# Attention probabilities turned by VectorE squares of 32 and DRAM transfers instead of by TensorE, from the fourth unit on

## The chip, the cores and the metric

One core of a Trainium2 chip runs the whole program. The metric is the device time of one execution in microseconds (us); lower is better. A time is the median of several runs; a profile is one execution recorded instruction by instruction.

## The reference

The program computes banded attention, and feeds its output to a gated feed-forward block with an RMS norm in front of it.

```python
# q, k, v: 8 batches x 8 heads x 576 rows x 64, float32
scores = (q @ k.T) / sqrt(64)
# heads 0-3: keep 0 <= rel < 32;  heads 4-7: keep 0 <= rel < 128 and rel % 4 == 0, with rel = row - key
attn = exp(scores - max);  attn = attn / (sum(attn) + 1e-9)
x = (attn @ v)                        # to 4608 tokens x 512
xn = x / sqrt(mean(x * x) + 1e-6) * rms_g
out = (silu(xn @ w_gate) * (xn @ w_val)) @ w_out      # 512 -> 1536 -> 512
```

## The kernel before, in words

**Units and bursts.** The 4608 tokens are cut into 16 units of 288 rows (half a sequence each, `U`). The attention of a unit is 14 bursts, `bursts(u)`: a burst is a pair of heads and a block of query rows. `geometry` gives its shape: pairs 0 and 1 (`c < 2`) have 3 blocks of 96 queries against 128 keys (96 keys for the first block of an even unit); pairs 2 and 3, the heads with dilation, have 4 blocks of 72 queries against 72 keys (even units) or 104 (odd units). From the fourth unit on (`u >= NEX`, 13 units, 182 bursts) the products of the attention are made in a high and a low part (float32r), so as to keep float32's accuracy.

**Steps.** The feed-forward block of a unit has 12 slices (`NJ`), and each slice three steps: `gate` (12 matmuls), `val` (12 matmuls) and `proj` of the slice before (12 matmuls). So a unit has 36 steps, and these matmuls fill TensorE. While unit u's feed-forward runs, the attention of unit u+1 is made in the gaps: `plan` writes down at which steps the parts of each burst go, and `attend` issues them behind the 12 matmuls of that step. From the fourth unit on the scores of burst k go at step -11 + 2k of the unit before, so one burst is started in every second step, 14 bursts in 28 of the 36 steps.

**What one burst does.** Let its scores be made at step s.

- s: `products` issues two score matmuls (L524) into the PSUM bank `s`.
- s+1: `scores_max` on VectorE: L381 adds the mask to the low part, L386 (twice) adds the rest and finds the maximum; the result is the tile `t`, 96 partitions x 2 heads x 128. The tag `t` has 3 buffers.
- s+2: `scores_exp` on ScalarE (L401), with the sums.
- s+4: `scores_norm`: two small operations on VectorE (L410, L411) and two multiplications on GpSimd (L417).
- s+6: two TensorE transposes (L497) into a free piece of a PSUM bank.
- s+7, s+8: `untranspose`: ScalarE copies the high part to the tile `pt` (L477), VectorE subtracts to get the low part (L479). The tag `pt` has 2 buffers.
- s+10: two output matmuls (L512) of `pt` with the parts of v into the bank `o`.
- s+11: `take` on VectorE (L439 and L441, twice each) adds the four pieces and moves them to `xraw`.

**What sets the order.** The schedule is manual: each engine runs its instructions in the order in which the program issues them. `later(dt, rank, fn)` puts a piece of work off by dt steps; `flush` at the start of a step issues what is due, sorted by rank; after it come the step's feed-forward matmuls and then `attend`. VectorE also carries two operations of each feed-forward slice (L724 behind `gate`, L737 behind `val`) in the same queue, and a `gate` two steps behind a `val` writes to that `val`'s PSUM bank, so it must wait for L737. All transfers are issued from one queue, SP's, in program order: `load` and `load_v` (L293, L301) for the next heads and value blocks, and the output (L777). A new tile in a slot waits until everything that used the tile before it in that slot is done, transfers included.

Of the kernel before, what the change touches and what calls it, by code (L numbers as in the profile page):

```python
# [20 lines left out]
P = 128  # L21
# [34 lines left out]
          2: (-3, -2, 0, 1, 3, 4, 6, 7, 9, 10, 12, 13, 15, 16)}  # L56

EARLY, LAST = -11, 15
BEHIND = 6, 10
DONE = 25  # L60


# [15 lines left out]
def attn_moe(ctx: ExitStack, tc: tile.TileContext, qk_in, v_in, w_gate, w_val, w_out, rms_g, outT):  # L78
# [6 lines left out]
    cst = ctx.enter_context(tc.tile_pool(name="cst", bufs=1))  # L85
    sb = ctx.enter_context(tc.tile_pool(name="sb", bufs=2))
    ps = ctx.enter_context(tc.tile_pool(name="ps", bufs=1, space=PSUM))


    ident = cst.tile([QB, QB], F32, name="ident")  # L90
# [29 lines left out]
    def later(dt, rank, fn):  # L120
        put_off.setdefault(now[0] + dt, []).append((rank, fn))
# [208 lines left out]
    def after(u, h, n):  # L330

        k = u * H + h + n
        return divmod(k, H) if k < NU * H else None
# [40 lines left out]
    def scores_max(u, c, i, s_ps):  # L374
        blocks, nq, _ = geometry(u, c)
        _, _, mc, n = blocks[i]
        sv = s_ps[:QB].rearrange("q (a t k) -> q a t k", a=2, t=2)
        other = u < NNAT and everything.index((u, c, i)) % 4 == 3
        t = sb.tile([QB, 2, P], F32, tag="qs" if other else "t", name=f"t_{u}_{c}_{i}", bufs=3)
        if u >= NEX:  # L380
            V.tensor_tensor(out=t[:nq, :, :n], in0=sv[:nq, :, 1, :n],  # L381
                            in1=mask[:nq, None, mc:mc + n].to_broadcast([nq, 2, n]), op=ALU.add)
        sm = sums[everything.index((u, c, i)) % len(sums)]
        for a in range(2):
            plus = t[:nq, a, :n] if u >= NEX else mask[:nq, mc:mc + n]
            V.tensor_tensor_reduce(out=t[:nq, a, :n], in0=sv[:nq, a, 0, :n], in1=plus,  # L386
                                   op0=ALU.add, op1=ALU.min,
                                   scale=-(0.5 if u == NNAT else 1.0) / math.sqrt(D),
                                   scalar=3e38, accum_out=sm[:nq, a, 0:1])
        st[u, c, i] = t, sm  # L390
# [77 lines left out]

    everything = [b for u in range(NU) for b in bursts(u)]

    def untranspose(b, t_ps, wait):
        blocks, nq, _ = geometry(*b[:2])
        n = blocks[b[2]][3]
        t_in = t_ps[:n].rearrange("k (a q) -> k a q", a=2)[:, :, :nq]
        exact = b[0] < NEX
        st[b] = pt = sb.tile([P, 2, 2, QB], F32 if exact else F32R, tag="pt", name=f"pt_{b[0]}_{b[1]}_{b[2]}", bufs=2)
        A.copy(out=pt[:n, 0, :, :nq], in_=t_in)  # L477
        def low_part():
            V.tensor_tensor(out=pt[:n, 1, :, :nq], in0=t_in, in1=pt[:n, 0, :, :nq], op=ALU.subtract)  # L479

        if not exact:
            later(1, 0.4 if wait > 1 else -1.5, low_part) if wait else low_part()

    def products(q, t, o, t_ps, s_tag="s", o_tag="o", wait=0):


        if q:
            s_ps = ps.tile([P, 512], F32, tag=s_tag, name=f"s_{q[0]}_{q[1]}_{q[2]}")
        if o:
            o_ps = ps.tile([P, 512], F32, tag=o_tag, name=f"o_{o[0]}_{o[1]}_{o[2]}")  # L490
            pt = st.pop(o)
        if t:
            p, _ = st.pop(t)
        def transposed(a):
            blocks, nq, _ = geometry(*t[:2])
            n = blocks[t[2]][3]
            PE.transpose(t_ps[:n, a * QB:a * QB + nq], p[:nq, a, :n], ident[:nq, :nq])  # L497

        def output(a):
            blocks, nq, _ = geometry(*o[:2])  # L500
            n = blocks[o[2]][3]
            if o[0] < NEX:
                if o[0] == 0:
                    PE.matmul(o_ps[a * D:(a + 1) * D, :nq], vs[o][:n, a], pt[:n, 0, a, :nq], start=True, stop=True)
                    return
                if a:
                    return
                out = o_ps[:, :2 * nq].rearrange("d (a q) -> d a q", a=2)
                PE.matmul(out, vs.pop(o)[:n].rearrange("k a d -> k (a d)"), pt[:n, 0, :, :nq], start=True, stop=True)  # L509
                return  # L510
            vp = vparts[everything.index(o) % 2]
            PE.matmul(o_ps[:, 2 * a * nq:2 * (a + 1) * nq].rearrange("d (t q) -> d t q", t=2),  # L512
                      vp[:n, a].rearrange("k t d -> k (t d)"), pt[:n, :, a, :nq], start=True, stop=True)

        def scored(a):
            blocks, nq, _ = geometry(*q[:2])
            qc, kc, _, n = blocks[q[2]]
            sv = s_ps[:QB].rearrange("q (a t k) -> q a t k", a=2, t=2)
            if q[0] < NEX:
                qk = heads[q[0], 2 * q[1] + a]  # L520
                PE.matmul(sv[:nq, a, 0, :n], qk[:, qc:qc + nq], qk[:, U + kc:U + kc + n], start=True, stop=True)  # L521
                return
            qs, ks = heads[q[0], 2 * q[1] + a]
            PE.matmul(sv[:nq, a, :, :n], qs[:, qc:qc + nq], ks[:, :, kc:kc + n], start=True, stop=True)  # L524

        order = ((t, transposed), (o, output), (q, scored))
        if t and t[0] >= NEX:
            order = ((o, output), (t, transposed), (q, scored))
        parts = [(b, fn, a) for b, fn in order for a in range(2)]
        for b, fn, a in parts:  # L530
            if b:
                fn(a)
        if t:
            later(1, 0.2, lambda: untranspose(t, t_ps, wait))
        if o:
            if o[0] < NEX or wait:
                later(1, 0.41 if o[0] < NEX else 0.55, lambda: take(*o, o_ps))
            else:
                for a in range(2):
                    later(1, (0.1, 0.3)[a], lambda a=a: take(*o, o_ps, (a,)))  # L540
            if o[0] < NEX:
                later(1, 9, lambda: load_v(further(o, 3)))
            far = further(o, 2)
            if far and far[0] >= NEX:
                split_v(far, 8 if o[0] < NEX else 1)
        if q:
            later(1, 0.7, lambda: scores_max(*q, s_ps))
            behind = q == (1, 0, 2)
            later(3 if behind else 2, 0.3 if behind else 0.42 if wait == 1 else 2, lambda: scores_exp(*q))
            later(3 if q[0] < NNAT else 4, 1 if behind else -1, lambda: scores_norm(*q))  # L550
            u, c, i = q
            nxt = after(u, 2 * c, 2)
            nb = len(geometry(u, c)[0])
            if u < NEX:
                if u == NNAT - 1 and c == NC - 1 and i == nb - 1:
                    for h in range(4):
                        later(1, 9, lambda h=h: load(NNAT, h))
                if u >= NNAT and i == nb - 1 and c < NC - 1:
                    for a in range(2):
                        later(1, 9, lambda a=a: load(*after(u, 2 * c + a, 4)))  # L560
                if u == NEX - 1 and c == NC - 1 and i == nb - 1:
                    for a in range(2):
                        later(3 + a, 9, lambda a=a: split(NEX, a, (1, 2, 2, 3), G, G))
            elif nxt and i == 0:
                split(*nxt, (1, 2, 2, 3), G, G)
                split(nxt[0], nxt[1] + 1, (2, 3, 3, 4) if c < NC - 1 else (1, 2, 3, 4), G, G)
# [241 lines left out]
    def plan(u, base, q_at, t_at, o_at):  # L808
        for b, *ts in zip(bursts(u), q_at, t_at, o_at):
            for kind, t in zip("qto", ts):  # L810
                events.setdefault(base + t, {})[kind] = b
        last = base + (o_at[-1] if u < NNAT else DONE)
        events.setdefault(last + (1, 4, 3)[min(u, 2)], {})["sum"] = u
        events.setdefault(last + (3, 7, 5)[min(u, 2)], {})["apply"] = u
# [13 lines left out]
    plan(0, 0, range(nb), range(LAG, nb + LAG), range(LAG + OUT, nb + LAG + OUT))  # L828
    for u in range(1, NU):
        q_at = [LAST - (LAST - EARLY) * (nb - 1 - k) // (nb - 1) for k in range(nb)]  # L830
        t_at, o_at = ([t + n for t in q_at] for n in BEHIND)
        if u <= NNAT:
            q_at = SCORES[u]
            t_at, o_at = [t + 5 for t in q_at], [t + (7 if u < NNAT else 8) for t in q_at]
        plan(u, ends - 2 + 3 * NJ * (u - 1), q_at, t_at, o_at)
# [22 lines left out]
    for u in range(NU):  # L858
        for j in range(NJ):
            for part in range(0 if u + j else 2, 3):  # L860
# [16 lines left out]
                else:  # L877
# [1 line left out]
                        proj(*prev)  # L879
                    prev = (u, j)  # L880
                    free = None
                if part == 2 or part == 1 and events.get(now[0], {}).get("t", (0,))[0] >= NEX:
                    if "t" in events.get(now[0], {}):
                        free = ps.tile([P, 512], F32, tag=bank("g", j), name=f"t_{u}_{j}")[:, :2 * QB]
                attend(free, s_tag="acc2" if t < 4 else "s", wait=(1, 2, 0)[part])
                now[0] += 1
    flush()
# [69 lines left out]
```

## Time and profile before

| | |
|---|---|
| median of 3 runs | 1104.47 us (1104.25 to 1106.05) |
| the profiled execution | 1103.95 us |
| its span, first to last instruction | 1102.2 us |
| TensorE matmul busy | 1095.2 us (99%) |
| VectorE busy | 782.7 us (71%) |
| ScalarE busy | 614.8 us (56%) |
| GpSimd busy | 670.1 us (61%) |
| transfers | 82.18 MB, 61543 packets |

In the profile PE is TensorE's matmuls, PEld its weight loads, DVE VectorE, ACT ScalarE, POOL GpSimd, SP the queue that issues transfers. A line such as `L381 DVE TENSOR_TENSOR t<-s,mask 96x256 f32<-96x256 f32 x66` names the source line, the engine, the operation, the tile written and the tiles read, the shapes and the count. In a timeline the first column is the start in us from the span's start and the second the duration; what stands in brackets is idle time of that engine just before, and what ended it. A window row gives busy time of each engine in a stretch, the granted clock of TensorE and the share of the transfer engines' time.

### The profile page before, as it was taken

Reading aid. Unit: us, or ns where it says so; the run is one execution under the profiler, and the core shown is the slowest. Engines: PE = TensorE matmul, PEld = TensorE weight load, DVE = VectorE, ACT = ScalarE, POOL = GpSimd, SP = SyncE. Lnnn points to the kernel's source line nnn. Section 1 sums busy time; section 2 is a strip of 40 time slices with the busy share of each in tenths; the row PEclk is TensorE's granted clock in tenths of the full one; section 3 lists DMA queues with packets and bytes.
Section 4 is the critical chain, followed back from the end, with each engine's and each line's share of the span. In section 5 each row is a group of like instructions: output and inputs, shape, how many; then the busy total and the mean of one; then the engine's idle time right before and its main releaser. Section 6 shows DMA issues by size and latency. Waiting matters only on the chain.

```text
span 1102.2 us, 25627 instructions
## 1 busy us (share of the span) xinstructions
PE 1095.2 (99%) x8416; PEld 1071.6 (97%) x8416; DVE 782.7 (71%) x3094; ACT 614.8 (56%) x2202; POOL 670.1 (61%) x1152
## 2 busy tenths in 40 slices
PE   8999999999999999999999999999999999999998
PEld 7787999999999999999999999999999999999998
DVE  7988667868687676867768677686867768687412
ACT  6895676556465564646556464664646556464211
POOL 6333589657585675757657575775758657584211
PEclk9999999999999999999999999999999999999999
DMA  9774213212131131312212131131212212120000
GB/s 255 205 263 163 79 51 87 74 35 82 43 94 52 41 97 30 95 42 73 66 36 85 43 94 43 50 96 37 79 43 83 64 32 83 53 74 13 18 6 22
DMA packets 61543, 82.18 MB, mean 75 GB/s; under 512 B 7298, under 2 KB 41090, under 8 KB 61410
## 3 DMA queue, kind: packets, MB, share of 16 engines
q1 hardware_dynamic: 61410, 80.54, 24.3%
q8 instruction: 67, 1.10, 0.4%
q14 instruction: 66, 0.54, 0.2%
HBM read 71.08 MB, written 9.44 MB: 73 GB/s over the span
## 4 chain that ended last, share of the span: by engine, by line
PE 95%; POOL 2%; DVE 1%; ACT 1%; issue 1%; POOLq 0%; ACTq 0%; DVEq 0%
PE acc L682 17%; PE g L682 17%; PE v L682 17%; PE acc L679 9%; PE g L679 9%; PE v L679 9%; PE o L512 3%; PE s L524 3%; PE acc L676 2%; PE v L676 2%; PE g L676 2%; PE t L497 2%; PE s L521 1%; PE g L497 1%; PE busy L802 1%; PE o L509 1%
## 5 line engine op out<-in xcount | busy, mean ns | idle before, releaser
L749 POOL TENSOR_TENSOR hlo<-th,hhi 128x288 fp32r<-128x288 f32 x179 | 145.2, 811 | 161.3 <-ACT hhi L748 147.8
L401 ACT ACTIVATE t<-t,sum 96x128 f32<-96x128 f32 (+3 forms) x448 | 165.9, 374 | 107.8 <-DVE sum L386 105.1
L682 PE MATMUL acc<-hhi,lo 128*128 128x288 f32 x720 | 212.7, 295 | 0.0
L417 POOL TENSOR_SCALAR t<-t,sum 96x128 f32<-96x128 f32 (+3 forms) x416 | 147.6, 366 | 88.4 <-DVE sum L411 74.6
L719 ACT ACTIVATE th<-g 128x288 f32<-128x288 f32 x180 | 73.8, 410 | 195.2 <-PE g L682 100.5
L682 PE MATMUL g<-xhi,lo 128*128 128x288 f32 x612 | 180.3, 295 | 0.0
L682 PE MATMUL v<-xhi,lo 128*128 128x288 f32 x612 | 180.2, 294 | 0.0
L439 DVE TENSOR_REDUCE xraw<-o 64x72 f32<-64x144 f32 (+1 forms) x364 | 117.1, 322 | 84.0 <-PE o L512 79.5
L724 DVE SCALAR_TENSOR_TENSOR th<-th,g 128x288 f32<-128x288 f32 x180 | 80.8, 449 | 102.0 <-ACT th L719 78.4
L682 PEld LDWEIGHTS acc<-hhi,lo 128*128 128x128 f32 x720 | 135.4, 188 | 0.0
L324 POOL TENSOR_TENSOR vhl<-vt,vhl 128x128 fp32r<-128x128 f32 x182 | 84.4, 464 | 70.4 <-ACT vhl L320 66.8
L748 ACT CAST hhi<-th 128x288 fp32r<-128x288 f32 x180 | 77.7, 432 | 75.5 <-DVE th L737 74.6
L682 PEld LDWEIGHTS g<-xhi,lo 128*128 128x128 f32 x612 | 115.2, 188 | 0.0
L682 PEld LDWEIGHTS v<-xhi,lo 128*128 128x128 f32 x612 | 115.1, 188 | 0.0
L737 DVE TENSOR_TENSOR th<-th,v 128x288 f32<-128x288 f32 x180 | 79.8, 444 | 43.6 <-PE v L682 43.5
L441 DVE TENSOR_TENSOR xraw<-o,xraw 64x72 f32<-64x72 f32 (+1 forms) x364 | 101.1, 278 | 12.5
L679 PE MATMUL acc<-hhi,hi_o 128*128 128x288 f32 x360 | 109.0, 303 | 0.0
L679 PE MATMUL g<-xhi,hi_g 128*128 128x288 f32 x357 | 107.0, 300 | 0.0
L682 PE MATMUL acc<-hlo,hi_o 128*128 128x288 f32 x360 | 106.4, 296 | 0.0
L363 POOL TENSOR_TENSOR qs<-qk,qs 64x288 fp32r<-64x288 f32 x104 | 84.3, 811 | 24.1 <-ACT qs L358 16.9
L354 POOL TENSOR_TENSOR ks<-qk,ks 128x288 fp32r<-128x288 f32 (+2 forms) x104 | 96.8, 936 | 3.1
L682 PE MATMUL g<-xlo,hi_g 128*128 128x288 f32 x322 | 95.1, 295 | 0.0
(193 smaller groups left out, 3458.6 us busy)
## 6 DMA issues: line engine op xcount, KB each, us to landing
qk<-in_qk_dram SPq DMA_DIRECT2D x60, 288.0 KB, 2.9
vt<-in_v_dram SPq DMA_DIRECT2D x196, 64.0 KB, 1.9
qk<-in_qk_dram SPq DMA_DIRECT2D x30, 352.0 KB, 2.9
out_dram<-ot SPq DMA_DIRECT2D x64, 144.0 KB, 1.9
qk<-in_qk_dram SPq DMA_DIRECT2D x30, 304.0 KB, 2.9
raw<-in_w_gate_dram SPq DMA_DIRECT2D x12, 512.0 KB, 4.6
raw<-in_w_val_dram SPq DMA_DIRECT2D x12, 512.0 KB, 3.3
raw<-in_w_out_dram SPq DMA_DIRECT2D x12, 512.0 KB, 4.2
```

What stands on the lines that cost most here:

```text
L324: G.tensor_tensor(out=vp[:, :, 1], in0=vs.pop(b), in1=vp[:, :, 0], op=ALU.subtract)
L354: ek.tensor_tensor(out=ks[:, 1, :nkt], in0=kr, in1=ks[:, 0, :nkt], op=ALU.subtract)
L363: eq.tensor_tensor(out=qs[D:], in0=qr[D:], in1=qs[D:], op=ALU.subtract)
L401: A.activation(out=t[:nq, a, :n], in_=t[:nq, a, :n], func=AF.Exp, scale=-1.0, bias=sm[:nq, a, 0:1], accum_out=None if by_rows(u, c, i) els ...
L417: (V if u == 0 and (c, i) > (NC - 1, 1) else G).tensor_scalar(out=t[:nq, a, :n], in0=t[:nq, a, :n], scalar1=sm[:nq, a, 3:4], scalar2=1.0, ...
L439: V.tensor_reduce(out=ours, in_=o[:D, cols:cols + 2 * nq].rearrange("d (t q) -> d q t", t=2), axis=mybir.AxisListType.X, op=ALU.add)
L441: V.tensor_tensor(out=ours, in0=o[D:, cols:cols + nq], in1=ours, op=ALU.add)
L679: PE.matmul(out, wh[:, cc, :], xh, start=start, stop=False)
L682: PE.matmul(out, w[:, cc, :], v, start=False, stop=stop and k == 1)
L724: V.scalar_tensor_tensor(out=t, in0=t, scalar=1.0, in1=g, op0=ALU.add, op1=ALU.mult)
L737: V.tensor_tensor(out=t, in0=t, in1=v_ps[:, :U], op=ALU.mult)
L749: (V if (u, j) == (NU - 1, NJ - 1) else G).tensor_tensor(out=lo, in0=t, in1=hi, op=ALU.subtract)
```

## The change

From the fourth unit on the two TensorE transposes of a burst, with their PSUM space, are gone. In their place stands `turn`, five pieces put off to fixed steps by `TURN`, counted from the step s of the scores:

- s+5: VectorE transposes the tile `t` in place, in squares of 32 x 32, over all 96 partitions and 256 columns.
- s+5, last in the step: three transfers on SP's queue ("put"), one for each 32 partitions of `t`, write the squares to their turned places in a DRAM tile `turn` of 128 x 2 x 96. Each has 256 runs of 128 bytes. The DRAM tile has 2 buffers.
- s+6, last in the step: one transfer on SP's queue ("get") reads the turned probabilities from DRAM into the low half of `pt`.
- s+9: ScalarE copies the high part, VectorE subtracts in place to get the low part. Both now read SBUF and not PSUM.

Since the squares cover all of `t`, a burst with fewer than 96 queries or 128 keys first has `t` filled with zeros by VectorE, in `scores_max` at s+1. Output matmuls stay at s+10. Units 0 to 2 keep the TensorE transposes.

```diff
-BEHIND = 6, 10
+OUTPUT = 10
+TURN = (5, 4), (5, 9.5), (6, 9.5), (9, 0.2), (9, 0.9)
...
+    dr = ctx.enter_context(tc.tile_pool(name="dr", bufs=2, space=bass.MemoryType.DRAM))
...
         if u >= NEX:
+            if nq < QB or n < P:
+                V.memset(t, 0.0)
             V.tensor_tensor(out=t[:nq, :, :n], in0=sv[:nq, :, 1, :n],
...
+    def turn(b):
...
+        def squares():
+            t = st[b][0]
+            V.transpose(out=t, in_=t)
+
+        def put():
+            t, _ = st.pop(b)
+            d = dr.tile([P, 2, QB], F32, tag="turn", name=f"turn_{b[0]}_{b[1]}_{b[2]}")
+            for r in range(QB // W):
+                nc.sync.dma_start(out=d[:, :, r * W:(r + 1) * W].rearrange("(c i) a j -> i a c j", i=W),
+                                  in_=t[r * W:(r + 1) * W].rearrange("i a (c j) -> i a c j", j=W))
+            got.append(d)
+
+        def get():
+            st[b] = pt = sb.tile([P, 2, 2, QB], F32R, tag="pt", name=f"pt_{b[0]}_{b[1]}_{b[2]}", bufs=2)
+            nc.sync.dma_start(out=pt[:n, 1, :, :nq].bitcast(F32), in_=got.pop()[:n, :, :nq])
+
+        def high():
+            pt = st[b]
+            A.copy(out=pt[:n, 0, :, :nq], in_=pt[:n, 1, :, :nq].bitcast(F32))
+
+        def low():
+            pt = st[b]
+            V.tensor_tensor(out=pt[:n, 1, :, :nq], in0=pt[:n, 1, :, :nq].bitcast(F32), in1=pt[:n, 0, :, :nq],
+                            op=ALU.subtract)
+
+        for (dt, rank), fn in zip(TURN, (squares, put, get, high, low)):
+            later(dt, rank, fn)
...
         order = ((t, transposed), (o, output), (q, scored))
-        if t and t[0] >= NEX:
-            order = ((o, output), (t, transposed), (q, scored))
...
             u, c, i = q
+            if u >= NEX:
+                turn(q)
...
-        t_at, o_at = ([t + n for t in q_at] for n in BEHIND)
+        t_at, o_at = [None] * nb, [t + OUTPUT for t in q_at]
```

More of the change, by code (lines that the diff above doesn't have):

```diff
@@ L469, in attn_moe, with untranspose @@
     everything = [b for u in range(NU) for b in bursts(u)]
-    def untranspose(b, t_ps, wait):
+    def untranspose(b, t_ps):
         blocks, nq, _ = geometry(*b[:2])
         n = blocks[b[2]][3]
[L474 to L482, printed above, removed]
+        st[b] = pt = sb.tile([P, 2, 2, QB], F32, tag="pt", name=f"pt_{b[0]}_{b[1]}_{b[2]}", bufs=2)
+        A.copy(out=pt[:n, 0, :, :nq], in_=t_ps[:n].rearrange("k (a q) -> k a q", a=2)[:, :, :nq])
+    def turn(b):
+        blocks, nq, _ = geometry(*b[:2])
+        n = blocks[b[2]][3]
+        got = []
+        def squares():
[20 more added lines that the diff above has]
+            later(dt, rank, fn)
     def products(q, t, o, t_ps, s_tag="s", o_tag="o", wait=0):
@@ L533, in products @@
         if t:
-            later(1, 0.2, lambda: untranspose(t, t_ps, wait))
+            later(1, 0.2, lambda: untranspose(t, t_ps))
         if o:
@@ L810, in plan @@
             for kind, t in zip("qto", ts):
-                events.setdefault(base + t, {})[kind] = b
+                if t is not None:
+                    events.setdefault(base + t, {})[kind] = b
         last = base + (o_at[-1] if u < NNAT else DONE)
@@ L881, in attn_moe @@
                     free = None
-                if part == 2 or part == 1 and events.get(now[0], {}).get("t", (0,))[0] >= NEX:
-                    if "t" in events.get(now[0], {}):
-                        free = ps.tile([P, 512], F32, tag=bank("g", j), name=f"t_{u}_{j}")[:, :2 * QB]
+                if part == 2 and "t" in events.get(now[0], {}):
+                    free = ps.tile([P, 512], F32, tag=bank("g", j), name=f"t_{u}_{j}")[:, :2 * QB]
                 attend(free, s_tag="acc2" if t < 4 else "s", wait=(1, 2, 0)[part])
```

## The prediction

> **What bounds the kernel now.** I read the page first: engine shares and the chain that ended last.
>
> ```profile
> span 1102.2 us, 25627 instructions
> PE 1095.2 (99%) x8416; PEld 1071.6 (97%) x8416; DVE 782.7 (71%) x3094; ACT 614.8 (56%) x2202; POOL 670.1 (61%) x1152
> PE 95%; POOL 2%; DVE 1%; ACT 1%; issue 1%; POOLq 0%; ACTq 0%; DVEq 0%
> ```
>
> TensorE sets the time, end to end: every nanosecond that leaves its queue is won, as long as nothing else comes to the front. An average of 71% for VectorE says little about stages, so next I cut one unit's 66 us (the tenth, typical) into windows: before the fourth burst's mask addition, from there to the fourteenth's, and the rest.
>
> ```profile
> 561.40:573.90 12.50, 12.50 (x101) 12.50 (x100) 8.57 (x34) 7.95 (x29) 8.41 (x15) 1.00 0.20 62
> 573.90:611.70 37.80, 37.80 (x304) 37.80 (x303) 31.19 (x136) 24.37 (x92) 29.82 (x51) 1.00 0.28 82
> 611.70:627.50 15.80, 15.80 (x126) 15.80 (x125) 9.56 (x36) 5.22 (x18) 6.32 (x12) 1.00 0.08 23
> ```
>
> The columns are PE, PEld, DVE, ACT, POOL busy, clock, DMA share, GB/s. In the middle window VectorE is busy 31.19 of 37.80 us. The change adds VectorE work just there, so its timeline decides:
>
> ```profile
> 589.34 0.36 DVE L381 TENSOR_TENSOR t<-s,mask 72x208 f32<-72x208 f32 x1
> 589.74 0.26 DVE L386 CUSTOM_DVE_ANT_0 t<-s,t 72x104 f32<-72x104 f32 x1
> ...
> 590.12 0.35 DVE L479 TENSOR_TENSOR pt<-g,pt 128x192 fp32r<-128x192 f32 x1
> 590.39 0.14 DVE L410 TENSOR_REDUCE sum<-sum 72x2 f32<-72x4 f32 x1
> 590.57 0.17 DVE L411 RECIPROCAL sum<-sum 72x2 f32<-72x2 f32 x1
> 590.65 0.43 DVE L737 TENSOR_TENSOR th<-th,v 128x288 f32<-128x288 f32 x1
> 591.40 0.35 DVE L439 TENSOR_REDUCE xraw<-o 64x96 f32<-64x192 f32 x1 [0.31 <-PE o L512]
> 591.78 0.26 DVE L441 TENSOR_TENSOR xraw<-o,xraw 64x96 f32<-64x96 f32 x1
> 592.07 0.36 DVE L479 TENSOR_TENSOR pt<-t,pt 128x192 fp32r<-128x192 f32 x1
> ...
> 593.14 0.37 DVE L381 TENSOR_TENSOR t<-s,mask 72x208 f32<-72x208 f32 x1
> ...
> 594.19 0.43 DVE L724 SCALAR_TENSOR_TENSOR th<-th,g 128x288 f32<-128x288 f32 x1
> 594.96 0.46 DVE L737 TENSOR_TENSOR th<-th,v 128x288 f32<-128x288 f32 x1 [0.33 <-PE v L682]
> ...
> 597.70 0.28 DVE L479 TENSOR_TENSOR pt<-t,pt 104x144 fp32r<-104x144 f32 x1
> 598.88 0.35 DVE L439 TENSOR_REDUCE xraw<-o 64x96 f32<-64x192 f32 x1 [0.90 <-PE o L512]
> ```
>
> VectorE runs nearly gapless and waits 0.31, 0.33 and 0.90 us in three bursts. One burst's `scores_max` takes 589.34 to 590.12, 0.78 us; one burst comes every 3.8 us (589.34, 593.14).
>
> **What it removes.** 182 pairs of transposes. Spacing of starts on TensorE:
>
> ```profile
> 591.00 0.36 PE L512 MATMUL o<-pt,vhl 128*128 128x192 f32 x2
> 591.20 0.33 PE L497 MATMUL t<-ident,t 96*128 96x96 f32 x2
> 591.31 0.41 PE L524 MATMUL s<-ks,qs 128*72 128x208 f32 x2
> 617.05 0.29 PE L497 MATMUL t<-ident,t 72*104 72x72 f32 x2
> 617.14 0.38 PE L679 MATMUL acc<-hhi,hi_o 128*128 128x288 f32 x1
> L497 PE MATMUL t<-ident,t 96*128 96x96 f32 (+3 forms) x262 | 40.4, 235 | 0.0
> ```
>
> A pair of 96 takes 0.11 us, a pair of 72 takes 0.09: 6 x 0.11 + 8 x 0.09 = 1.4 us a unit, 18 us over 13 units. The group's busy time, 40.4 / 262 = 0.154 us each, would make it 56 us; but that counts modelled ends under which the next matmul already runs, so I take the spacing. `untranspose`'s two operations become `high` and `low` with the same shapes: no change in count, SBUF for PSUM as source. I cost that at nothing; VectorE's low part keeps 0.31 us with its gap, as the mean of the rows above.
>
> **What it adds on VectorE.** The squares: 96 x 256 elements. No transpose by VectorE is in the trace; the nearest rows are single operations over 256 columns and the zero fill at the start:
>
> ```profile
> L409 DVE TENSOR_REDUCE sum<-t x11: 293/300/418, 7.1 to 24.3; 72x2 f32<-72x144 f32 x7, 96x2 f32<-96x192 f32 x2, 96x2 f32<-96x256 f32 x2
> L263 DVE MEMSET qk<- x3: 538/538/538, 0.9 to 2.1; 64x576 f32 x3
> ```
>
> The 256-column form is the longest, 0.418 us; with the usual gap 0.03 I take 0.45. Bounds: 0.30 (the median row) and 0.84 (twice the longest, if squares need two passes). The Trainium skill, "VectorE: DVE Perf Modes", section "The three transpose paths", gives VectorE 311 ns for a 128 x 128 bf16 transpose; an estimate from it with 128 more columns at 0.96 GHz is 0.44 us, which would raise the sum by 3 us. The zero fill: between 0.24 (0.538 x 256 / 576) and 0.42; I take 0.27 and a gap, 0.30. It is needed in all dilated bursts.
>
> **What it adds as a wait.** This decides. The tag `t` has 3 buffers. Burst k's `t` is read by put at s+5, and the tile of burst k+3, written from s+7 on, has the same slot. Before, the reader was TensorE at s+6. Now `scores_max` of k+3 must wait until put of k has landed in DRAM. Queued behind it on VectorE: L737 and L724 of the feed-forward, the `low` of k-1, the squares of k+1; TensorE waits for all of them, through PSUM banks and `pt`. From the squares of k to the next squares VectorE therefore needs, in this order: landing of put (L), fill and `scores_max` of k+3, `low` of k-1, squares of k+1. Norm, `take` and feed-forward operations (about 2.2 us) lie under L. The loop's period is
>
> - dilated: L + 0.30 + 0.78 + 0.31 + 0.45 = L + 1.84
> - 96 queries: L + 0.85 + 0.38 + 0.45 = L + 1.68
>
> (no fill; 0.78 + 0.07, since its mask addition below takes 0.41 and not 0.36, and an allowance for the two L386; 0.35 + 0.03 for its low part.)
>
> L is three issues in a row on SP and the landing of the third:
>
> ```profile
> 586.40 2.05 SPq L777 DMA_DIRECT2D out_dram<-ot  x4
> L777 SPq DMA_DIRECT2D out_dram<-ot x64: 332/425/1857, 119.4 to 1099.5; - x64
> DMA to landing us min/median/max: 1.8/1.9/3.7
> q1 hardware_dynamic: 61410, 80.54, 24.3%
> qk<-in_qk_dram SPq DMA_DIRECT2D x60, 288.0 KB, 2.9
> ```
>
> Output transfers are the kernel's only writes to DRAM: 0.425 us to issue, 1.9 us from issue to landing; four in a row take 2.05 us, 0.54 from start to start at most. So L = 2 x 0.45 + 1.9 + 0.15 for the wake-up of SP and of VectorE (an estimate, about two of the small gaps around SP's issues) = 2.95 us. From below: 2 x 0.33 + 1.8 = 2.5. From above: 2 x 0.43 + 2.9 (a larger transfer's landing) = 3.7.
>
> The period is then 4.79 us dilated and 4.63 otherwise, against the 3.8 of today. The get is no second bound: it is issued when put has landed, lands 1.9 us later, and is needed four steps after the squares, two periods. SP's queue has room: put, landing, get and one value load make 2.95 + 2 x 0.43 = 3.8 us a period. Behind put and get stand the loads of values and heads; SP holds them back today already, until GpSimd frees their buffers, so a delay of a period costs nothing as long as they land before their splits:
>
> ```profile
> SPq L301 <- POOL vhl L324: 347.2, 128, 4.2
> ```
>
> If that cover goes, ScalarE waits for a load.
>
> **The sum.**
>
> ```profile
> 573.92 0.41 DVE L381 TENSOR_TENSOR t<-s,mask 96x256 f32<-96x256 f32 x1
> 611.65 0.36 DVE L381 TENSOR_TENSOR t<-s,mask 72x208 f32<-72x208 f32 x1
> ```
>
> From the fourth to the fourteenth mask addition of a unit, ten periods, took 37.7 us. Now: 3 x 4.63 + 7 x 4.79 = 47.4. That is 9.7 us more. Off it goes the lead that VectorE has over TensorE, spent once a unit: the low part ended at 590.47, TensorE's output matmul began at 591.00, 0.5 us. Transposes outside the ten periods (bursts 0, 11, 12, 13) are still won, 0.4 us; those inside are not, since TensorE waits there. So 9.7 - 0.5 - 0.4 = 8.8 us a unit, and 13 units make 114 us. Against the profiled execution, 1103.95 us (span 1102.2, the rest around it; 0.5 under the median), that is **1218 us**, slower by 10%. With L = 2.5, squares 0.30 and fill 0.24 the ten periods are 41.5 us: +2.9 a unit, 1142. With L = 3.7 and the other terms as taken: 54.9, +16.3 a unit, 1316.
>
> **Rivals.**
>
> - *VectorE alone.* Put lands while VectorE is still busy; the limit is VectorE's own work. The middle window has 31.19 us busy and about 3 us of small gaps (some 100 of 0.03); ten squares and eight fills add 6.9: 41, 3.3 more than 37.7. Less the 0.9 as above: 2.4 x 13 = 31, 1135 us. For it: the 0.31 and 0.90 us waits show how little room there is. Against: L would have to be under 2.2 us, with one transfer alone taking 1.9.
> - *Faster.* The mechanism is the removed 1.4 us a unit on TensorE, with nothing in its place: 1103.95 - 18 = 1086 us. It decides where the period stays under 3.6 us: L below 1.8, or squares and fill far cheaper than any row. For it: 1.5 us of idle time in three bursts on VectorE. Against: three transfers cannot land sooner than one.
> - *Slow put.* The put pays for each of its 768 runs. The q1 row gives a mean of 24.3% x 1102.2 x 16 / 61410 = 0.070 us a packet, 48 packets to an engine: 3.4 us if each costs the mean, on top of 1.9 for the landing and 0.15: L = 5.45, ten periods 72.4, +33.8 a unit, 1543 us. At half that price L is 3.75 and the time 1322. Against: packets here average 1311 bytes, ten times these runs. The Trainium skill, "DMA: Bandwidth & Descriptors", section "Specifications", says that transfers under 512 B do not reach line rate since the engine reads, modifies and writes; by that rule this rival gains, and no row here shows such a write.
>
> **How the numbers follow.** Forecast 0.62; VectorE alone 0.13; slow put 0.15; faster 0.07; no change that can be measured (within 0.2%, about what a measurement of this kernel can tell) 0.03. The range must hold the forecast's 1142 to 1316 and reach into the slow put's near part and just below VectorE alone: 1120 to 1370. All cases but these two are slower: 0.90; faster 0.07, same 0.03.
>
> **What would show it.** In the profile after: a VectorE transpose in 182 copies of about 0.42 us; 116 zero fills; VectorE waiting for a transfer to `turn` ahead of the fill or the mask addition, some 0.7 us a burst, 90 us or more in all; TensorE's share down to about 88% with its waits on VectorE ahead of output or score matmuls; mask additions 4.6 to 4.8 us apart inside the ten periods; three puts issued about 0.45 us apart. Wrong would be: VectorE without such waits (then the limit is its own work or nothing), or ScalarE held at `high` by the get, or squares under 0.3 us.

## The result and the profile after

| | before | after |
|---|---|---|
| median of 4 runs | 1105.12 us (1104.25 to 1106.05) | 1387.2 us (1383.24 to 1388.96) |
| the profiled execution | 1103.95 us | 1388.96 us |
| ratio after / before | | 1.2547, 95% interval 1.2518 to 1.2577 |

The change costs 25%. The prediction had the sign and the main loop, 1218 us with a range to 1370; the time lies above the range. The profiled execution is 285 us longer, where 114 were forecast: 171 us are to be explained.

The page after: span, busy time of each engine, and the chain that ended last by engine and by line.

```profile
span 1387.2 us, 27102 instructions
...
PE 1167.7 (84%) x8052; PEld 1103.1 (80%) x8052; DVE 875.5 (63%) x3392; ACT 620.1 (45%) x2202; POOL 667.8 (48%) x1152
...
DMA 26%; DVE 26%; PE 25%; SPq 9%; issue 6%; POOL 4%; ACT 3%; DVEq 1%; POOLq 0%; ACTq 0%
DMA turn<-t 23%; SPq L494 9%; PE g L712 4%; DVE t L385 4%; DMA pt<-turn 3%; DVE t L488 3%; PE v L712 3%; PE acc L712 3%; DVE pt L508 3%; DVE t L390 3%; PE g L709 3%; DVE t L384 2%; DVE th L767 2%; DVE th L754 2%; PE v L709 2%
```

The chain was 95% TensorE. Now TensorE is a quarter of it, and the put (its landing, `DMA turn<-t` 23%, and its issue, `SPq L494` 9%) a third. VectorE did 93 us more work than before and is busy for a smaller share: it waits. The waits, in us in total, times and longest:

```profile
PE o L542 <- DVE pt L508: 180.2, 126, 2.9
DVE t L384 <- DMA turn<-t: 174.5, 110, 3.4
...
ACT pt L504 <- DMA pt<-turn: 136.0, 100, 4.6
...
DVE t L385 <- DMA turn<-t: 52.5, 32, 3.8
```

Rows two and four are the forecast wait for a buffer of `t`, 227 us in 142 waits: eleven a unit, where the prediction counted ten periods. Row one is what TensorE makes of it: the output matmuls wait for the low part. Row three is the sign that the prediction had listed under "wrong": ScalarE held at `high` by the get.

The tenth unit, cut as before (before the fourth mask addition, from there to the fourteenth, the rest; columns as in the prediction):

```profile
694.90:707.30 12.40, 12.40 (x98) 12.36 (x96) 7.32 (x30) 7.46 (x26) 9.07 (x16) 1.00 0.27 73
707.30:762.50 55.20, 39.01 (x280) 36.08 (x278) 36.80 (x151) 23.93 (x89) 28.10 (x49) 1.00 0.36 89
762.50:783.90 21.40, 17.16 (x116) 16.62 (x117) 12.70 (x46) 6.42 (x22) 7.57 (x14) 0.94 0.20 42
```

The middle window grew from 37.80 to 55.20 us while VectorE's busy time in it grew by 5.6 only. The last grew from 15.8 to 21.4, and TensorE has idle time there as well.

For all units the starts of the mask addition (L385) give three stretches: the head, from a unit's first to its fourth; the ten periods, from the fourth to the fourteenth; the tail, from the fourteenth to the next unit's first. Means in us, here and in all tables below:

| | ten periods | head | tail | one unit |
|---|---|---|---|---|
| before | 37.6 | 10.9 | 17.5 | 66.0 |
| after | 54.6 | 12.9 | 20.5 | 88.0 |
| more | 17.0 | 2.0 | 3.0 | 22.0 |
| forecast more | 9.7 | together -0.9 | | 8.8 |

Times 13 units, the 7.3 us missed in the ten periods make 94 of the 171 us, and the 5.9 us outside make 77: 26 in the head, and 51 in the tail with the 0.9 that was to be won.

**One period.** VectorE's timeline from one zero fill to the next:

```profile
734.57 0.27 DVE L384 MEMSET t<- 96x256 f32 x1 [1.83 <-DMA turn<-t]
734.94 0.37 DVE L385 TENSOR_TENSOR t<-s,mask 72x208 f32<-72x208 f32 x1
...
735.72 0.35 DVE L508 TENSOR_TENSOR pt<-pt 128x192 fp32r<-128x192 f32 x1
735.99 0.43 DVE L488 STREAM_TRANSPOSE t<-t 96x256 f32<-96x256 f32 x1
...
738.52 0.26 DVE L445 TENSOR_TENSOR xraw<-o,xraw 64x96 f32<-64x96 f32 x1
739.90 0.27 DVE L384 MEMSET t<- 96x256 f32 x1 [1.12 <-DMA turn<-t]
```

It is the loop that the prediction wrote down, in its order: fill, mask addition, low part, squares, put, landing, fill. 739.90 - 734.57 = 5.33 us, where 4.79 stood. The same stretch in SP's timeline:

```profile
736.46 1.88 SPq L494 DMA_DIRECT2D turn<-t  x3
739.78 0.88 SPq L500 DMA_DIRECT2D pt<-turn  x1
740.70 0.52 SPq L303 DMA_DIRECT2D vt<-in_v_dram  x1
```

The squares end at 736.42 and SP starts the put at once. Three issues take 1.88 us, not 3 x 0.43. The get starts at 739.78, when the third put has landed. So from the squares' end to the landing it is 3.3 us. TensorE meanwhile waits for the low part:

```profile
736.22 0.44 PE L542 MATMUL o<-pt,vhl 128*128 128x192 f32 x2 [1.19 <-DVE pt L508]
```

The operations over the whole run, first by the tile `turn`, then by the tile `t`: ns (minimum, median, maximum), first and last start:

```profile
L494 SPq DMA_DIRECT2D turn<-t x546: 569/608/1968, 178.4 to 1303.0; - x182
L500 SPq DMA_DIRECT2D pt<-turn x182: 325/825/962, 181.9 to 1305.0; - x182
```

```profile
L488 DVE STREAM_TRANSPOSE t<-t x182: 429/434/439, 176.4 to 1300.6; 96x256 f32<-96x256 f32 x182
L384 DVE MEMSET t<- x116: 272/272/272, 198.2 to 1291.0; 96x256 f32 x116
```

Squares (0.434) and fill (0.272) came out as taken. A put's issue is 0.61 us, and in the trace's transfer records the starts lie 0.63 to 0.65 apart; the third put lands 1.97 us after its issue (median of 182). The get's issue has two sizes, 0.33 and 0.82 to 0.88.

**The tail.** Bursts are counted from 0 here. The squares of burst 12 come 2.5 us (median) after those of burst 11, and here SP is the limit. Its timeline, then ScalarE's waits for the get in the same stretch:

```profile
772.19 0.87 SPq L500 DMA_DIRECT2D pt<-turn  x1
773.11 0.52 SPq L303 DMA_DIRECT2D vt<-in_v_dram  x1
773.68 1.90 SPq L494 DMA_DIRECT2D turn<-t  x3
777.84 0.87 SPq L500 DMA_DIRECT2D pt<-turn  x1
```

```profile
769.87 0.31 ACT L504 CAST pt<-pt 104x144 fp32r<-104x144 f32 x1 [2.55 <-DMA pt<-turn]
774.63 0.31 ACT L504 CAST pt<-pt 104x144 fp32r<-104x144 f32 x1 [2.64 <-DMA pt<-turn]
780.33 0.31 ACT L504 CAST pt<-pt 104x144 fp32r<-104x144 f32 x1 [4.21 <-DMA pt<-turn]
```

SP issues the put (1.90 us), then stands at the get until the put has landed, and only then comes the next burst's put. The squares of bursts 12 and 13 are done 2.4 and 2.7 us (medians over the units) before their put is issued.

### The profile page after: what moved, and what is told of

Read it like the earlier page. It is cut to its first block, busy times and chain, and to the rows that moved or that the text cites. A ratio compares the mean times of both kernels' runs of the same rounds, so it can differ in the third digit from the quotient of the medians.

```text
span 1387.2 us, 27102 instructions
## 1 busy us (share of the span) xinstructions
PE 1167.7 (84%) x8052; PEld 1103.1 (80%) x8052; DVE 875.5 (63%) x3392; ACT 620.1 (45%) x2202; POOL 667.8 (48%) x1152
## 4 chain that ended last, share of the span: by engine, by line
DMA 26%; DVE 26%; PE 25%; SPq 9%; issue 6%; POOL 4%; ACT 3%; DVEq 1%; POOLq 0%; ACTq 0%
DMA turn<-t 23%; SPq L494 9%; PE g L712 4%; DVE t L385 4%; DMA pt<-turn 3%; DVE t L488 3%; PE v L712 3%; PE acc L712 3%; DVE pt L508 3%; DVE t L390 3%; PE g L709 3%; DVE t L384 2%; DVE th L767 2%; DVE th L754 2%; PE v L709 2%
## 5 line engine op out<-in xcount | busy, mean ns | idle before, releaser
L542 PE MATMUL o<-pt,vhl 128*128 128x192 f32 (+3 forms) x364 | 75.7, 290 | 180.2 <-DVE pt L508 180.2
L542 PEld LDWEIGHTS o<-pt,vhl 128*128 128x128 f32 (+3 forms) x364 | 55.9, 190 | 207.6 <-issue 156.2
L712 PE MATMUL g<-xhi,lo 128*128 128x288 f32 x612 | 188.8, 308 | 0.0
L712 PE MATMUL v<-xhi,lo 128*128 128x288 f32 x612 | 186.9, 305 | 0.0
L384 DVE MEMSET t<- 96x256 f32 x116 | 31.6, 272 | 175.2 <-DMA turn<-t 174.5
L712 PEld LDWEIGHTS g<-xhi,lo 128*128 128x128 f32 x612 | 123.3, 201 | 0.0
L712 PEld LDWEIGHTS v<-xhi,lo 128*128 128x128 f32 x612 | 122.2, 200 | 0.0
L504 ACT CAST pt<-pt 128x192 fp32r<-128x192 f32 (+3 forms) x182 | 59.4, 327 | 136.4 <-DMA pt<-turn 136.0
L709 PE MATMUL g<-xhi,hi_g 128*128 128x288 f32 x357 | 114.5, 321 | 6.2 <-DVE th L767 6.1
L385 DVE TENSOR_TENSOR t<-s,mask 96x256 f32<-96x256 f32 (+3 forms) x182 | 67.2, 369 | 66.4 <-DMA turn<-t 52.5
```

Source lines behind the costliest of these rows:

```text
L385: V.tensor_tensor(out=t[:nq, :, :n], in0=sv[:nq, :, 1, :n], in1=mask[:nq, None, mc:mc + n].to_broadcast([nq, 2, n]), op=ALU.add)
L709: PE.matmul(out, wh[:, cc, :], xh, start=start, stop=False)
L712: PE.matmul(out, w[:, cc, :], v, start=False, stop=stop and k == 1)
```

## The experiments

The theory after the result: the buffer of `t` that waits for the put bounds the head and the ten periods, with a longer issue than forecast; SP's order put, landing, get, next put bounds the tail. The rivals: VectorE's own work; the get, that is ScalarE at `high`; TensorE's lowered clock. Each time is that of one profiled execution, beside one of the kernel before on the same chip (1103.95 us for the first four, 1105.53 for the next four, 1104.1 for the last four), so no step of a time under 10 us is built upon; the stretches are means over the units.

| | time, us | ten periods | head | tail |
|---|---|---|---|---|
| after | 1388.96 | 54.6 | 12.9 | 20.5 |
| e1: four buffers of `t` | 1313.9 | 46.2 | 10.8 | 25.0 |
| e2: e1, get later | 1304.6 | 47.7 | 10.7 | 23.1 |
| e3: one put, not three | 1232.9 | 45.6 | 12.6 | 17.8 |
| e4: no squares | 1317.0 | 49.8 | 12.8 | 19.9 |
| e5: before, with VectorE's new work | 1151.0 | 40.7 | 10.9 | 17.9 |
| e6: TensorE's idle time filled | 1400.0 | 54.9 | 12.7 | 21.1 |
| e7: squares and put first in their step | 1262.2 | 46.7 | 13.0 | 18.5 |
| e8: e1 and e7 | 1231.1 | 43.6 | 11.1 | 21.1 |
| e9: get in whole rows | 1363.2 | 54.1 | 12.6 | 19.3 |
| e10: e8, e9, get just ahead of the next put | 1191.1 | 43.6 | 11.2 | 17.8 |
| e11: e10, fill and norm off VectorE | 1189.4 | 43.2 | 11.1 | 18.2 |
| e12: e11, low part off VectorE | 1182.8 | 42.7 | 11.2 | 18.0 |

**e1: take the buffer wait away.** Every fourth burst's `t` gets a slot of its own, so that burst k+4 and not k+3 waits for put k; the space comes from the value blocks, which have two buffers in place of three and are loaded two bursts ahead. Kernels e2, e8 and e10 to e12 have this too, and no run has it alone.

```diff
-            vt = sb.tile([P, 2, D], F32, tag="vt", name=f"vt_{u}_{c}_{i}", bufs=3)
+            vt = sb.tile([P, 2, D], F32, tag="vt", name=f"vt_{u}_{c}_{i}", bufs=2)
...
-            load_v(further(b, 3))
+            load_v(further(b, 2))
...
-        t = sb.tile([QB, 2, P], F32, tag="qs" if other else "t", name=f"t_{u}_{c}_{i}", bufs=3)
+        if u >= NEX and everything.index((u, c, i)) % 4 == 3:
+            t = late[0].tile([QB, 2, P], F32, tag="t4", name=f"t_{u}_{c}_{i}", bufs=1)
+        else:
+            t = sb.tile([QB, 2, P], F32, tag="qs" if other else "t", name=f"t_{u}_{c}_{i}", bufs=3)
```

> A fourth buffer for the tile t from the fourth unit on (room for it: two buffers for the value blocks in place of three, loaded two bursts ahead in place of three). Theory (VectorE's scores_max of burst k+3 waits in the slot of t until put of burst k has landed, 3.3 us after the squares, and this sets a period of 5.3 us): the waits on turn ahead of the zero fill and the mask addition, 227 us in all, fall to under 30 us, and the next limit shows: SP, which holds put, its landing and get in series (3.3 + 0.9 + value load 0.4 = 4.6 us a burst); ten periods near 47 us in place of 54.6, about 1290 us. Rival (VectorE's own work is the limit and its waits on transfers only fill its idle time): 1370 to 1390 us, no change.

Measured: 1313.9 us, 75 less; the waits and the ten periods (46.2) are as expected, the time is 24 us above. First the rows of those who waited for the tile `turn` (the lines of this kernel are three further down), then a row of the waits:

```profile
  ACT pt L507: 471.8, 176
...
  DVE t L387: 5.1, 6
```

```profile
PE o L545 <- DVE pt L511: 146.8, 146, 3.3
```

VectorE's wait for a landing fell from 227 to 5 us, and the head went back to 10.8: that wait did bound the head and the ten periods. SP's waits for a free value block stayed as they were (52 us before this edit, 54 with it). But ScalarE's wait for the get rose from 136 to 472 us and the tail to 25.0, and TensorE goes on waiting for the low part: a second limit, near the first, took over.

**e2: four buffers, the get where the put has long landed.** In e1's kernel the get is moved one step back, so that SP does not stand at it.

```diff
-TURN = (5, 4), (5, 9.5), (6, 9.5), (9, 0.2), (9, 0.9)
+TURN = (5, 4), (5, 9.5), (7, 9.3), (9, 0.2), (9, 0.9)
```

> As the one with four buffers of t, and get one step later, just ahead of the next put, so that SP no longer stands still between put and get. Theory: with both holds gone VectorE's own work is the limit, about 4.1 us a burst, ten periods near 41 us, 1130 to 1170 us. Rival (SP's issue time or the transfers' throughput is the limit): above 1250 us. Rival (get lands too late for ScalarE's high part): waits of ScalarE on pt<-turn of over 100 us and a time above 1200 us.

Measured: 1304.6 us, far from 1130 to 1170; the theory that only VectorE's work would be left falls here, and the rival of the late get is borne out. The time is also above the 1250 us from which on the rival of SP's issue time holds; this run does not part the two. ScalarE and SP's queue:

```profile
ACT pt L507 <- DMA pt<-turn: 479.7, 182, 5.2
```

```profile
SPq L303 <- POOL vhl L326: 214.8, 166, 3.1
```

ScalarE stands at `high` for 480 us. Behind that stands its split of the values, so GpSimd frees the value block late, the load of the next block on SP waits for GpSimd (215 us), and behind that load waits the put, 1.84 us (median) after its squares. So the queues seem to form a ring, in which SP's order is not a matter of the get alone; that the two value buffers have no part in it is not shown.

**e3: one transfer for the put.** It writes the same bytes in whole rows. It leaves out the move of the squares to their turned places, so it shows what the three issues cost and is no version to use.

```diff
-            for r in range(QB // W):
-                nc.sync.dma_start(out=d[:, :, r * W:(r + 1) * W].rearrange("(c i) a j -> i a c j", i=W),
-                                  in_=t[r * W:(r + 1) * W].rearrange("i a (c j) -> i a c j", j=W))
+            nc.sync.dma_start(out=d.rearrange("p a j -> (p a j)").rearrange("(q x) -> q x", x=2 * P),
+                              in_=t.rearrange("q a k -> q (a k)"))
```

> Put is one transfer of 96 runs of 1024 bytes in place of three of 256 runs of 128 bytes; the squares land in the wrong places, so the turned probabilities are not those of the reference; bytes, squares, buffers and waits are the same. Theory: the landing of put seen from the end of the squares falls from 3.3 to about 2.0 us (two issues of 0.64 us less), the period from 5.3 to 4.1 us, where VectorE's own work begins to limit; 1180 to 1240 us. Rival (the short runs' own price makes the put slow): the landing of a single put, 1.97 us from its issue, would fall well below 1.9 us. Rival (VectorE's own work alone): 1370 to 1390 us.

Measured: 1232.9 us, 156 less, within what was expected. The put's issue, and VectorE's wait at the fill:

```profile
L493 SPq DMA_DIRECT2D turn<-t x182: 303/331/1262, 177.3 to 1143.5; - x182
...
  DVE t L384: 65.3, 60
```

One put of 331 ns instead of three of 608 takes the 1.27 us between the first and the third out of the loop; the ten periods fell by 9.0 us of the 12.7 that this alone would give, the tail by 2.7. So three short-run puts in place of one long-run put cost 156 of the 285 us, the most that any single edit of the changed kernel gave back; the prediction had their issue at 0.45 each. The gains of e1, e3, e4 and e7 must not be added up, since all four loosen the same loop. The sign of the rival with a price of short runs in the landing is not there: from the put's start to that of its get, which waits for the landing, it is 2.3 us (median), against 2.1 from the third put of the kernel after.

**e4: no squares.** One edit, `-            V.transpose(out=t, in_=t)`.

> The squares by VectorE are left out; put moves the tile as it is, so the turned probabilities are not those of the reference. Theory (squares stand in the loop of the slot of t): each period falls by 0.43 us, 10 x 0.43 x 13 = 56 us, about 1330 us. Rival (the limit is a wait on transfers in which VectorE's work is hidden): under 15 us.

Measured: 1317.0 us, 72 less, where 56 were expected. The ten periods fell by 4.7 us, 0.47 a period: the squares lie in the loop at their full price of 0.43 and a gap.

**e5: VectorE's new work without the transfers.** The kernel before, with the fill and the squares added; TensorE's transposes stay.

```diff
         if u >= NEX:
+            if nq < QB or n < P:
+                V.memset(t, 0.0)
             V.tensor_tensor(out=t[:nq, :, :n], in0=sv[:nq, :, 1, :n],
...
+            if u >= NEX:
+                later(5, 4, lambda: V.transpose(out=st[q][0], in_=st[q][0]))
```

> The kernel before, TensorE's transposes and all, with only the change's new VectorE work added from the fourth unit on: the zero fill, and the squares in place one step before TensorE's transposes, so that the probabilities used are not those of the reference. No transfer is added. Theory (VectorE's own work is the smaller part of the loss): ten periods near 41 us in place of 37.7, 1140 to 1160 us. Rival (VectorE's work is most of the loss and the transfers only add idle time to it): over 1250 us. Rival (it fits into VectorE's idle time): under 1112 us.

Measured: 1151.0 us, 45 above its own kernel before. The engines, and the group of the squares:

```profile
PE 1119.7 (97%) x8416; PEld 1079.9 (94%) x8416; DVE 871.8 (76%) x3392; ACT 613.9 (53%) x2202; POOL 671.1 (58%) x1152
...
L555 DVE STREAM_TRANSPOSE t<-t 96x256 f32<-96x256 f32 x182 | 79.3, 436 | 0.8
```

VectorE does within 4 us the work of the kernel after (871.8 and 875.5 us) and the ten periods take 40.7, where the rival "VectorE alone" had 41. So of the 285 us some 45 are VectorE's own work. The prediction's 18 us for the transposes would come off that, but no run measured them by themselves; by difference, the other 240 to 258 us are the way through DRAM.

**e6: the clock.** Six small matmuls into a piece of PSUM ahead of the output matmuls of nine of a unit's 14 bursts (702 matmuls more in all), to keep TensorE from standing idle.

```diff
+        if o and o[0] >= NEX and fill is not None:
+            for _ in range(6):
+                PE.matmul(fill, ones, ones[:, None, :64].to_broadcast([P, 3, 64]), start=True, stop=True)
```

> The changed kernel with six needless matmuls of 192 columns ahead of the output products of a burst in two of three steps that have them, where TensorE waits for VectorE, so that the record of its granted clock shows fewer stretches at half. The matmuls' results are not used. Theory (the clock's drops are a follower of the waits, and most of the slower matmuls lie where TensorE would wait anyway): granted clock up from 0.958 to over 0.98, time within 15 us of the changed kernel, 1370 to 1400 us. Rival (the drops are a cause of the excess over the forecast): 34 drops of 3.4 us at half cost up to 58 us, so the time falls to 1330 to 1350 us.

Measured: 1400.0 us, and the granted clock hardly moved (0.961 against 0.958 after and 1.000 before), so the expected 0.98 was missed and this does not tell the clock's price. In the profile after the clock falls to half 34 times, for 3.4 us each; in the kernel before once, outside these stretches. 28 of the 34 lie within the ten periods, where the loop through VectorE and SP adds up to the period without TensorE. The window rows of the tenth unit bear that out: its ten periods had the full clock throughout (1.00) and yet took 55.2 us, no less than the mean of 54.6. The six outside can cost at most 6 x 1.7 = 10 us. The Trainium skill, "TensorE: Matmul & The Clock Gate", section "What's actually happening", gives the gate an activity window of 3413 ns; the 3.4 us agree with that. In the trace all 34 stretches start on one grid of 3.413 us, and in the step of that grid just ahead of each TensorE was idle for 47% to 80% of the time (by the modelled ends of its matmuls); of the other 301 steps between 150 us from the start and 90 us from the end, none was idle for more than 52%. Before the stretches of e6 the share is as high (46% to 80%), so its six matmuls did not fill the steps that mattered.

**e7: squares and put at the front of their step.** Three buffers as in the change, only the order differs: squares first, the put right behind, and the parts later in their step.

```diff
-TURN = (5, 4), (5, 9.5), (6, 9.5), (9, 0.2), (9, 0.9)
+TURN = (5, 0.6), (5, 0.61), (6, 9.5), (9, 3.5), (9, 4.5)
```

> The changed kernel with other ranks alone, three buffers of t: squares and put stand behind take and ahead of scores_max in their step (put ahead of the value load on SP), and the high and low parts stand last in theirs, so ScalarE and VectorE meet them later. Theory (two latencies bound the changed kernel in turn: the slot of t waits for put, and the parts wait for get, with SP's order between them): with the squares no longer between the landing and the next put, two periods hold one landing, and get has some 1.5 us more; ten periods fall from 54.6 to under 45 us, 1180 to 1250 us. Rival (SP's issues and landings in series bound it, about 4.7 us a burst): 1290 us or more.

Measured: 1262.2 us, 127 less without a byte or an instruction changed. It missed what was expected, 1250 us at most and ten periods under 45 (they take 46.7), and is also under the rival's 1290. VectorE's wait for `turn` fell from 227 to 85 us (63.3 and 21.5), ScalarE's for the get from 136 to 69. Our reading is that, with the squares ahead of the low part and of the rest of the step, the landing starts earlier against the fill that needs it. SP is nearer to being the limit here: the put starts 1.47 us (median) after its squares, against 0.03 in the kernel after.

**e8: e1's buffers and e7's order.**

> The same ranks and the fourth buffer of t. Theory: with the slot's wait gone as well, what remains is the chain of put and get against the parts, and VectorE's work: 1130 to 1200 us, below the one with three buffers. Rival (SP in series): no more than 15 us below the one with three buffers and both above 1280 us.

Measured: 1231.1 us. Both expectations missed: neither did VectorE's work alone stay, nor were the buffers worth under 15 us beyond e7, but 31. The ten periods are at 43.6; the tail is 21.1, and ScalarE waits 198.4 us for the get.

**e9: the get in whole rows.** For the dilated bursts the get reads 72 of 96 columns, two pieces a row. Here it reads the row whole, padding included.

```diff
-            nc.sync.dma_start(out=pt[:n, 1, :, :nq].bitcast(F32), in_=got.pop()[:n, :, :nq])
+            nc.sync.dma_start(out=pt[:, 1].bitcast(F32), in_=got.pop())
```

> The changed kernel, but get reads whole rows of turn, 128 of 768 bytes, in every burst; the changed kernel reads 72 or 104 rows in two pieces in dilated bursts, which takes 0.88 us to issue and lands after 2.45 us against 0.33 and 1.9. Theory (inside the ten periods put's landing and the slot of t set the pace, outside them put, get and parts in series): ten periods stay within 1 us of 54.6, the gain lies outside them, and the time is 1350 to 1380 us. Rival (get against the parts sets the pace throughout): 1.1 us a burst less, over 100 us, under 1290 us.

Measured: 1363.2 us, as expected: the tail 1.3 and the head 0.4 us shorter, the ten periods 0.5. The get, and who waits:

```profile
L500 SPq DMA_DIRECT2D pt<-turn x182: 325/332/335, 182.4 to 1279.2; - x182
...
  DVE t L384: 168.2, 110
  ACT pt L504: 91.3, 74
```

The issue is 0.33 us for all bursts, with more bytes: the two pieces of a row cost 0.5 us of SP's time. The get also lands sooner, 1.95 us (median) after its start against 2.4. The two together are 26 us of the loss. VectorE's wait is as it was (168 against 174.5), so the get is a second limit beside the first.

**e10: all of it, with the get put off.** e8's buffers, e9's get, and the get just ahead of the next burst's put, so that SP should seldom stand at it.

```diff
-TURN = (5, 4), (5, 9.5), (6, 9.5), (9, 0.2), (9, 0.9)
+TURN = (5, 0.6), (5, 0.61), (7, 0.3), (9, 3.5), (9, 4.5)
```

> Four buffers of t, squares and put ahead of scores_max, get of whole rows one step later and ahead of the next put, parts last in their step. Theory: SP never stands still for a landing and ScalarE meets a get that has landed, so VectorE's own work is left, which alone gave 1151 us with TensorE's transposes: 1130 to 1170 us. Rival (some landing still bounds it, or TensorE and ScalarE wait on the short chain): over 1190 us.

Measured: 1191.1 us, above the expected 1130 to 1170 and at the edge of the rival's 1190. The tail, 25.0 and 21.1 with four buffers in e1 and e8, is back at 17.8, near the 17.5 of the kernel before: what it had lost is SP's time and the get, in its issue, landing and place. The ten periods stay at 43.6, against 40.7 for VectorE's work alone. The engines, the longest wait for a transfer, and SP's wait at the get:

```profile
PE 1106.5 (93%) x8052; PEld 1054.3 (89%) x8052; DVE 905.2 (76%) x3392; ACT 624.5 (53%) x2202; POOL 670.4 (56%) x1152
```

```profile
ACT pt L507 <- DMA pt<-turn: 134.5, 127, 2.5
```

```profile
SPq L503 <- DMA turn<-t: 114.3, 158, 2.4
```

TensorE is at 93% and VectorE at 76%, and ScalarE still waits for the get as long in all as in the kernel after (136.0). The theory that SP never stands still for a landing did not hold: it stood at the get for 114 us (196 in the kernel after), and the put starts 2.05 us (median) after its squares.

**e11 and e12: relieve VectorE.** In e11 GpSimd fills `t` and ScalarE does the two multiplications of the norm; in e12 GpSimd also makes the low part.

```diff
+        if u >= NEX and (nq < QB or n < P):
+            G.memset(t, 0.0)
...
-            if u == 1:
+            if u == 1 or u >= NEX:
```

> As the kernel with get ahead of the next put, and VectorE relieved: the zero fill by GpSimd at the start of the step, the multiplication by the inverse sum by ScalarE in place of GpSimd. Theory (VectorE's work bounds): 0.30 us less in 8 of 14 bursts, 13 x 8 x 0.3 = 31 us below that kernel. Rival (landings bound it): no more than 8 us below it.

```diff
-            V.tensor_tensor(out=pt[:n, 1, :, :nq], in0=pt[:n, 1, :, :nq].bitcast(F32), in1=pt[:n, 0, :, :nq],
+            G.tensor_tensor(out=pt[:n, 1, :, :nq], in0=pt[:n, 1, :, :nq].bitcast(F32), in1=pt[:n, 0, :, :nq],
```

> As the one before, with the subtraction for the low part by GpSimd too. Theory: VectorE then carries 0.1 us more a burst than in the kernel before, TensorE 1.4 us less a unit, so the time is near the kernel before's: 1085 to 1125 us. Rival (ScalarE and GpSimd, or the chain of put and get, take VectorE's place): no gain on the one before.

Measured: 1189.4 and 1182.8 us. Both miss, and both rivals hold: 1.6 us and 6.6 us are too small to build on. VectorE's busy time fell from 905 in e10 to 875 and 828 us, so its load alone is not what holds e10, though ScalarE's rose from 625 to 722 and 716. e12's waits:

```profile
POOL pt L519 <- ACT pt L515: 197.2, 114, 3.8
...
ACT pt L515 <- DMA pt<-turn: 114.2, 106, 3.8
...
PE o L553 <- POOL pt L519: 57.8, 68, 3.1
```

In the low part's place stands its wait for `high`, and behind that `high`'s wait for the get: the chain squares, put, landing, get, landing, high, low, output matmul still ends late in many bursts, at s+10 as before. What would shorten it (a later output matmul, with a third `pt`) was not tried. No version came under the kernel before.

## Why the prediction was right in its direction and wrong in its size

- **The loop.** Right, term for term, in its members and their order. The wait at `turn` was forecast at 90 us or more; it was 227, and e1 shows it to be the buffer's.
- **VectorE's prices.** Squares 0.434 us (0.42 forecast), fill 0.272, and 0.47 a period for taking the squares out (e4). These stand. The rival "VectorE alone" had the ten periods at 41; e5 measured 40.7.
- **The first failed step: "So L = 2 x 0.45 + 1.9 + 0.15".** The landing was right, 1.97 for 1.9. The issue was mis-sized: 0.45 came from rows of output transfers (whose four in a row already started 0.54 apart at most), where a put with 256 runs of 128 bytes takes 0.61 and the next starts 0.64 later. That is 2 x 0.19 = 0.4 us a period. The rest of the 5.33 against 4.79, about 0.15, is the landing's 0.07 and the wake-ups, 0.22 in this period where 0.15 was estimated; VectorE's own part, from the fill to the end of the squares, took 1.85 us where 1.84 was forecast. Some periods are longer still (the last but one of a unit has a median of 6.1 us, since the put of the tenth burst lands after 2.4 us; that other transfers are in its way is likely and not shown), so that the mean is 5.46. Over the ten periods that is 7.3 us, 94 in all. The upper bound for L, 3.7, covered it: it gave 54.9 us for the ten periods, and 54.6 were measured. That is luck: this bound has a longer landing (2.9) and issues of 0.43, where the issues were longer and the landing was not.
- **The count of the waits.** The sum began at the fourth mask addition. But the fourth burst's own fill waits too, for the put of the first, and that wait lies in the head: the eleventh of a unit. It costs 2.0 us, 26 in all, and is gone in e1.
- **The second failed step: "The get is no second bound ... SP's queue has room".** It was reckoned for periods of 4.8 us and with issues of 0.43. In the tail the squares of burst 12 come 2.5 us after those of burst 11, and SP's own round is put, landing, get and load, 3.3 + 0.9 + 0.5 = 4.7 us. The squares of bursts 12 and 13 stand ready 2.4 and 2.7 us there and ScalarE is held at `high`: 3.0 us more a unit where 0.9 were to be won, 51 in all. This and the eleventh wait took the time out of the range. e9 (26 us for the get's issue and landing) and e10 (the tail back at 17.8) bear it out; e2 shows that SP also stands behind GpSimd.
- **The slow put.** Its sign, a later landing, isn't there: 1.97 us with 128-byte runs, 1.9 for the output's. The Trainium skill, "DMA: Bandwidth & Descriptors", section "Specifications", has transfers under 512 B miss line rate; no such loss shows in the landing of these 32 KB. What these runs cost is seen in SP's issue (0.61 us, against 0.33 for the one long-run put of e3), which that rival did not have.
- **TensorE.** 84% busy, 88% forecast, and the waits at the output matmuls as named. The 18 us for the transposes were not measured by themselves.
- **Open.** What holds e10 to e12 50 to 58 us above 1151 - 18 = 1133 us is not shown. ScalarE's wait for the get (112 to 134 us) and SP's wait at it (114 us in e10) are left, but no run took them away, and the load moved to ScalarE and GpSimd is not ruled out. The price of the half clock is bounded by the trace alone (six stretches outside the ten periods, and a unit without any), not by a run.

## What to carry to other kernels

When a step within a pipeline of few buffers is given to transfers, write the loop of the buffer and the loop of the issuing queue side by side, each for the place where the work comes closest together, not for its mean: here the first gave 5.3 us and the second 4.7, and bursts came every 3.8 and, at a unit's end, once after 2.5. Price a transfer's issue by a row with the same run length, and take the next limit as near as the first: removing the buffer wait (e1) gave back 75 us of 285. Before adding buffers, try the order: moving squares and put to the front of their step was worth 127 us. And count the issues: one put in place of three (e3, which leaves the turn undone) was worth 156.

## What the runs showed of the hardware that was not expected

- The issue time of a transfer on SP depended more on its pattern than on its bytes: 0.33 us for whole rows (e3's put of 96 KB, e9's get of 96 KB), 0.61 for 32 KB in 256 runs of 128 bytes, 0.82 to 0.88 for a get of 72 of 96 columns in two pieces a row. In the pair of e9 the larger transfer was the cheaper by 0.5 us.
- The 128-byte runs did not land later: 1.97 us from the issue (32 KB), against 1.9 for the output transfers of the kernel before (144 KB).
- TensorE's granted clock fell to half for 3.4 us 34 times in a kernel that kept it 84% busy, with waits of at most 2.9 us. Each time TensorE had been idle for about half or more (47% to 80%) of the 3.413 us just before. Six small matmuls ahead of nine of 14 bursts did not prevent it.
